# Attention steps with both batches in the same swapped halves, and a weight conversion in two parts

## The chip, the core and the metric

The kernel runs on one core of a Trainium2 chip. Times are device microseconds of one execution; a lower time is better. A core has five engines with queues of their own: PE (TensorE, matmuls, with PEld for its weight loads), DVE (VectorE), ACT (ScalarE), POOL (GpSimd) and SP (SyncE, which issues most DMAs here).

## The reference

Three stages follow each other; all tensors are float32.

```
# linear attention with decay: 2 batches, 8 heads, 12 blocks of 64 positions, head_dim 64
for b in range(12):
    intra = (q_b @ k_b^T * Dmask) @ v_b                # Dmask[i,j] = lam^(i-j) for i >= j
    out_b = intra + (q_b * lam^(pos+1)) @ kv_state
    kv_state = lam^64 * kv_state + (k_b * lam^(63-pos))^T @ v_b
x = out, as 1536 tokens x 512
h = x @ w_in;  x = max(0.01*h, h) @ w_out              # 512 -> 2048 -> 512
h = x @ w_in2                                          # 512 -> 1024
solu = h * softmax(h);  ln = (solu - mean) / sqrt(var + 1e-6) * g_ln
return ln @ w_out2                                     # 1024 -> 512
```

The weights come to the kernel as 64-bit words, which it turns into float32 on the chip.

## The kernel before

Attention is cut into 12 steps, one per block of 64 positions, each for both batches (b = 0, 1). The 8 heads of a batch lie as 4 pairs, the two heads of a pair in the two halves of the 128 partitions. So every attention matmul is 64x64: four of them fit into the 128x128 array at once, one per quadrant (row half of the operands, column half of the output). A step has four kinds, 16 matmuls of each: *scores* (k, q; L169) of the next step, evicted by DVE with the decay mask as r; *xs* (v, r; L201) and *xq* (state, scaled q; L210), which add up in one bank to the step's output x; and *state* (k, v; L183), which DVE adds to the decayed state. On the feature side head h of batch 0 lies in half 1-h, of batch 1 in half h (`d_rows`, L86), so that the same matmul of both batches together fills four quadrants. xs uses two quadrants of one diagonal in each batch; xq of batch 0 writes the rows of xs from other partitions, hence a `pe.drain()` between them (L240).

Steps 0 to 3 run at the start (from L485), one kind after the other. Steps 4 to 11 stand inside the main loop (L561), which goes through 48 units (b, f): three blocks of 512 tokens by 16 slices of w_in and w_out. In unit i PE runs `l1_mm` (w_in, 12 matmuls 128x128 by 512, into a bank hps), the step if i is 4, 7, 10, 13, 17, 21, 25 or 29, and then `l2_mm` of unit i-1 (w_out, 12 matmuls into acc). Matmuls are done in split precision: an operand has a high and a low piece, and the 12 matmuls of `l1_mm` are four with both high pieces, four with the low piece of x, four with the low piece of the weight (L348), in this order. `l1_split` makes Prelu (ACT, L353), the high piece ghi (ACT, L356) and the low piece glo (DVE, L357).

In units 1 to 15 and 35 to 44 the weights of later units are made ready as well. For a weight n: `words` (ACT, L291 and L292) takes two parts out of the 64-bit words; `convert` (DVE, L300 to L302) limits, shifts and joins them to the float32 x; `high` (ACT, L322) rounds x to its high piece and `low` (DVE, L340) subtracts. Unit i does high and low of weight i+1, convert of i+2, words of i+3 and the load of i+5. `scale_k`, `scale_q` and `decay_state` multiply with powers of the decay, on POOL inside the loop.

Each engine runs its instructions in the order in which the program is written (L625 makes that a dependency), so a waiting instruction holds back all behind it on its engine. DMAs go through eight semaphores in turn: a DMA is issued when the eighth before it has landed.

Of the kernel before, what the change touches and what calls it, by code (L numbers as in the profile page):

```python
# [16 lines left out]
P = 128  # L17
CH = 64
NPAIR = 4
NB = 2  # L20
# [21 lines left out]
def fused_kernel(ctx: ExitStack, tc: tile.TileContext, att, vt, tab, cst, w_in, w_out, w_in2, w_out2, out):  # L42
# [42 lines left out]

    def d_rows(b, h):  # L86
        return HALF[h if b else 1 - h]

# [15 lines left out]
    def load_step(s):  # L104

        t = wp.tile([P, 2048], F32, tag="w", name="ldw")
        qkk = t[:, 0:1536].rearrange("p (n c a b) -> p n c a b", n=NB, c=3, a=NPAIR)
        v = t[:, 1536:2048].rearrange("p (n a b) -> p n a b", n=NB, a=NPAIR)
        second = act if s == 0 else sync
        sync.dma_start(out=qkk[:, 0], in_=att[2 * s])  # L110
        for h, queue in ((0, second), (1, sync)):
            queue.dma_start(out=qkk[HALF[h], 1, 0:2], in_=att[2 * s + 1][HALF[1 - h], 0:2])
        second.dma_start(out=v, in_=vt[s])
        sync.dma_start(out=qkk[:, 1, 2], in_=att[2 * s + 1][:, 2])
        ld[s] = (qkk[:, :, 0], qkk[:, :, 1], qkk[:, :, 2], v)

    qk_t = {}

    def load_qk(s):
        if s >= NS:  # L120
            return
        t = qk_t[s] = ap2.tile([P, NB, 2, NPAIR, CH], F32, tag="qk", name="qk")
        sync.dma_start(out=t[:, 0], in_=att[2 * s][:, 0:2])
        for h in range(2):
            sync.dma_start(out=t[HALF[h], 1], in_=att[2 * s + 1][HALF[1 - h], 0:2])

    def load_kv(s):
        if s >= NS:
            return
        t = ap1.tile([P, 2, NB, NPAIR, CH], F32, tag="kv", name="kv")  # L130
        sync.dma_start(out=t[:, 0], in_=att[2 * s : 2 * s + 2, :, 2].rearrange("n p a b -> p n a b"))
        sync.dma_start(out=t[:, 1], in_=vt[s])
        ld[s] = (qk_t[s][:, :, 0], qk_t[s][:, :, 1], t[:, 0], t[:, 1])
# [21 lines left out]
    def decay_state(s, eng):  # L155

        if not 0 < s < NS - 1:
            return
        sd_t[s] = ap1.tile(SHAPE, F32, tag="sd", name="sd")
        n = NB * NPAIR  # L160
        dec = qpow.rearrange("p n a b -> p (n a) b")[:, :, CH - 1 : CH].to_broadcast([P, n, CH])
        st, out_ = (t.rearrange("p n a b -> p (n a) b") for t in (s_t[s], sd_t[s]))
        eng.tensor_tensor(out_, st, dec, op=ALU.mult)

    def scores_mm(s, bank, b, pr):
        q, k = (qk_t[s][:, :, 0], qk_t[s][:, :, 1]) if s >= NPRE else ld[s][0:2]
        for h in range(2):
            d = d_rows(b, h)
            pe.matmul(at(bank, HALF[h], b, pr), k[d, b, pr], q[d, b, pr], start=True, stop=True)  # L169

# [8 lines left out]
    def state_mm(s, bank, b, pr):  # L179

        for h in range(2):
            j = HALF[h]
            pe.matmul(at(bank, d_rows(b, h), b, pr), ld[s][KJ][j, b, pr], ld[s][V][j, b, pr], start=True, stop=True)  # L183

# [11 lines left out]
    def xs_mm(s, bank, b, pr):  # L196

        first = pr == 0 and (b == 0 or isinstance(bank, tuple))
        for h in range(2):
            j = HALF[h]  # L200
            pe.matmul(  # L201
                at(bank, j, b, pr), ld[s][V][j, b, pr], r_t[s][j, b, pr], start=(s == 0 or first), stop=(s == 0)
            )

    def xq_mm(s, bank, b, pr):

        last = pr == NPAIR - 1 and (b == 0 or isinstance(bank, tuple))
        for h in range(2):
            d = d_rows(b, h)
# [9 lines left out]

    def scores(s, bank):  # L220
        each_pair(*((scores_mm, s, bank, b) for b in range(NB)))

    def state(s, bank):
        each_pair(*((state_mm, s, bank, b) for b in range(NB)))

    def x_early(s, bank):
        for b in range(NB):
            each_pair((xs_mm, s, bank, b))
        if s > 0:
            pe.drain()  # L230
            each_pair(*((xq_mm, s, bank, b) for b in range(NB)))

    def step(s, xbank, kbank, rbank):


        more, state_too = s + 1 < NS, s < NS - 1
        each_pair((xs_mm, s, xbank, 0), *([(state_mm, s, kbank, 0)] if state_too else []))
        each_pair((xs_mm, s, xbank, 1), *([(scores_mm, s + 1, rbank, 0)] if more else []))
        each_pair((xq_mm, s, xbank, 1))
        pe.drain()  # L240
        each_pair((xq_mm, s, xbank, 0), *([(state_mm, s, kbank, 1)] if state_too else []))
        if more:
            each_pair((scores_mm, s + 1, rbank, 1))

    def scores_alone(s, rbank):
        each_pair((scores_mm, s, rbank, 0))
        pe.drain()
        each_pair((scores_mm, s, rbank, 1))

# [17 lines left out]

    def load_weights(n):
        if n >= len(order):
            return  # L270
        kind, f = key = order[n]
        t = wp.tile([P, 2, 512, 2], U32, tag="w", name="raww")
        if kind == "a":
            sync.dma_start(out=t.rearrange("p h a b -> p (h a b)"), in_=w_in2[f].bitcast(U32))
        else:
            for i, src in enumerate((w_in[f], w_out[f]) if kind == "io" else (w_out2[f], w_out2[f + 1])):
                sync.dma_start(out=t[:, i].rearrange("p a b -> p (a b)"), in_=src.bitcast(U32))
        raws[n] = t

    BOTH = slice(0, 2)
# [11 lines left out]
    def convert(n, halves=BOTH):  # L294
        if n >= len(order):
            return
        raw = raws[n][:, halves].rearrange("p h a b -> p (h a) b")
        x = xs_t[n][:, halves].rearrange("p h a -> p (h a)")
        xu = x.bitcast(U32)
        dve.tensor_scalar(x, x, HI_MAX, -HI_MAX, op0=ALU.min, op1=ALU.max)  # L300
# [174 lines left out]
    for pr in range(NPAIR):  # L475
        lamj = lams[:, 0, pr : pr + 1].to_broadcast([P, CH])
        dve.tensor_tensor_scan(dmask[:, pr], lamj, delta[:, pr], 0.0, op0=ALU.mult, op1=ALU.add)
    for b in range(NB):
        for pr in range(NPAIR):
            lamd = lams[:, 1 - b, pr : pr + 1].to_broadcast([P, CH])  # L480
            dve.tensor_tensor_scan(qpow[:, b, pr], lamd, zero, 1.0, op0=ALU.mult, op1=ALU.add)
# [3 lines left out]
    scale_k(0, pool)  # L485
    scores(0, sb)
    scores_ev(0, sb)
    state(0, kb)
    x_early(0, xb[0])
    state_ev(0, kb)  # L490
# [9 lines left out]
    scale_k(1, act)  # L500
    scores(1, sb)
    scores_ev(1, sb)
    x_early(1, xb[1])
    state(1, kb)
    low(0, IN)
# [8 lines left out]
    decay_state(2, pool)  # L514
    scores(2, sb)
    scores_ev(2, sb)
    low(0, OUT)
    scale_q(3, pool)
    x_early(2, xb[0])
    scores(3, sb)  # L520
    state(2, kb)
    scores_ev(3, sb)
# [5 lines left out]
    words(1, OUT)  # L528
    x_early(3, xb[1])
    decay_state(3, pool)  # L530
# [6 lines left out]
    l1_mm((0, 0), hps[0])  # L537
    state(3, sb)
    convert(1, OUT)
# [21 lines left out]
    for i, u in enumerate(items[1:], 1):  # L561
# [4 lines left out]
        if i == 2:  # L566
            scores_alone(NPRE, spare)
# [119 lines left out]
```

## Time and profile before

| | |
|---|---|
| three runs | 466.72, 466.94, 468.98 us; median 466.94 |
| the profiled execution | 467.06 us, span 465.3 us |
| PE busy | 449.8 us, 97% |
| DVE busy | 262.1 us, 56% |
| ACT busy | 187.2 us, 40% |
| POOL busy | 53.3 us, 11% |
| chain that ended last | PE 90%, DMA 3%, DVE 3%, ACT 1%, issue 1% |

A busy PE is not PE at its peak: the share says only that some matmul was under way. The chain of waits is followed back from the last instruction, at each step to what released it; its shares say what the time went through. Rows of the timeline merge instructions of one kind that follow each other; two rows may overlap.

### The profile page before, as it was taken

Reading aid. Unit: us, or ns where it says so; the run is one execution under the profiler, and the core shown is the slowest. Engines: PE = TensorE matmul, PEld = TensorE weight load, DVE = VectorE, ACT = ScalarE, POOL = GpSimd, SP = SyncE. Lnnn points to the kernel's source line nnn. Section 1 sums busy time; section 2 is a strip of 40 time slices with the busy share of each in tenths; the row PEclk is TensorE's granted clock in tenths of the full one; section 3 lists DMA queues with packets and bytes.
Section 4 is the critical chain, followed back from the end, with each engine's and each line's share of the span. In section 5 each row is a group of like instructions: output and inputs, shape, how many; then the busy total and the mean of one; then the engine's idle time right before and its main releaser. Section 6 shows DMA issues by size and latency. Waiting matters only on the chain.

```text
span 465.3 us, 7890 instructions
## 1 busy us (share of the span) xinstructions
PE 449.8 (97%) x3332; PEld 370.8 (80%) x3332; DVE 262.1 (56%) x417; ACT 187.2 (40%) x311; POOL 53.3 (11%) x57
## 2 busy tenths in 40 slices
PE   6788999999999999999999999999999999999997
PEld 3765788888888888888888888888888888888886
DVE  4697899999832121211131888912877666666651
ACT  3657667557332222122244777622322222222221
POOL 2434041240403030100000000000000000000000
PEclk9798999999999999999999999999999999999999
DMA  8999064931302020100015542000000000000001
GB/s 273 337 350 370 4 229 173 323 118 66 92 0 93 1 92 1 46 0 2 1 48 213 191 180 92 0 0 2 0 24 23 24 23 23 24 23 24 23 24 45
DMA packets 16659, 41.61 MB, mean 89 GB/s; under 512 B 1904, under 2 KB 4976, under 8 KB 16112
## 3 DMA queue, kind: packets, MB, share of 16 engines
q1 hardware_dynamic: 16400, 40.71, 24.9%
q8 instruction: 26, 0.43, 0.4%
q10 hardware_dynamic: 224, 0.39, 0.3%
q14 instruction: 9, 0.07, 0.0%
HBM read 37.95 MB, written 3.15 MB: 88 GB/s over the span
## 4 chain that ended last, share of the span: by engine, by line
PE 90%; DMA 3%; DVE 3%; ACT 1%; issue 1%; SPq 0%; ACTq 0%
PE hps L350 28%; PE acc L366 27%; PE acc L446 14%; PE hps L384 7%; PE aps L384 7%; DMA ldw<-in_att_dram 3%; PE acc L424 2%; PE aps L210 2%; PE aps L201 2%; PE hps L169 1%; DVE raww L301 1%; DVE x L302 1%; ACT wio L322 0%; DVE xlo L260 0%; DVE state L194 0%
## 5 line engine op out<-in xcount | busy, mean ns | idle before, releaser
L350 PE MATMUL hps<-xhi,wio 128*128 128x512 f32 x384 | 104.0, 393 | 3.2 <-ACT wio L322 2.2
L357 DVE TENSOR_TENSOR glo<-hps,ghi 128x512 fp32r<-128x512 f32 x48 | 33.2, 691 | 122.5 <-ACT ghi L356 121.2
L366 PE MATMUL acc<-ghi,wio 128*128 128x512 f32 x384 | 96.0, 392 | 0.0
L350 PEld LDWEIGHTS hps<-xhi,wio 128*128 128x128 f32 x384 | 72.3, 189 | 19.2 <-ACT wio L322 2.6
L353 ACT ACTIVATE hps<-hps 128x512 f32<-128x512 f32 x48 | 28.0, 582 | 143.4 <-PE hps L350 143.4
L366 PEld LDWEIGHTS acc<-ghi,wio 128*128 128x128 f32 x384 | 71.4, 188 | 15.1
L350 PE MATMUL hps<-xlo,wio 128*128 128x512 f32 x192 | 52.3, 395 | 1.2 <-DVE xlo L260 1.2
L366 PE MATMUL acc<-glo,wio 128*128 128x512 f32 x192 | 51.3, 389 | 0.0
L446 PE MATMUL acc<-wb,lnhi 128*128 128x512 f32 (+1 forms) x208 | 46.0, 374 | 0.3 <-ACT lnhi L432 0.3
L350 PEld LDWEIGHTS hps<-xlo,wio 128*128 128x128 f32 x192 | 36.5, 191 | 9.4 <-DVE xlo L260 1.7
L446 PEld LDWEIGHTS acc<-wb,lnhi 128*128 128x128 f32 x208 | 36.9, 188 | 7.4 <-ACT lnhi L432 0.6
L366 PEld LDWEIGHTS acc<-glo,wio 128*128 128x128 f32 x192 | 36.1, 188 | 7.5
L416 POOL TENSOR_TENSOR small<-small,nhalf 128x1 f32<-128x1 f32 x12 | 6.6, 548 | 251.7 <-DVE small L415 243.3
L301 DVE SCALAR_TENSOR_TENSOR raww<-x,raww 128x1024 uint32<-128x1024 uint32 (+1 forms) x26 | 32.0, 1231 | 1.2 <-ACT raww L292 0.3
L302 DVE SCALAR_TENSOR_TENSOR x<-x,raww 128x1024 uint32<-128x1024 uint32 (+1 forms) x26 | 31.6, 1214 | 0.9
L291 ACT ACTIVATE x<-raww 128x1024 f32<-128x1024 f32 (+1 forms) x26 | 27.9, 1073 | 2.2 <-DMA raww<-in_w_in_dram 2.2
L356 ACT CAST ghi<-hps 128x512 fp32r<-128x512 f32 x48 | 28.2, 587 | 1.5
L292 ACT ACTIVATE raww<-raww 128x1024 uint32<-128x1024 uint16 (+1 forms) x26 | 28.0, 1077 | 0.0
L141 POOL TENSOR_TENSOR qk<-qk,qpow 128x512 f32<-128x512 f32 x8 | 12.2, 1525 | 122.5 <-PE hps L169 122.5
L384 PE MATMUL hps<-wa,xhi 128*128 128x512 f32 x96 | 24.2, 394 | 0.0
L384 PE MATMUL aps<-wa,xhi 128*128 128x512 f32 x96 | 24.2, 394 | 0.0
L446 PE MATMUL acc<-wb,lnlo 128*128 128x512 f32 (+1 forms) x104 | 24.0, 373 | 0.0
(82 smaller groups left out, 527.1 us busy)
## 6 DMA issues: line engine op xcount, KB each, us to landing
raww<-in_w_out_dram SPq DMA_DIRECT2D x24, 512.0 KB, 6.8
raww<-in_w_in_dram SPq DMA_DIRECT2D x16, 512.0 KB, 6.8
raww<-in_w_in_dram SPq DMA_DIRECT2D x4, 1024.0 KB, 4.8
out_dram<-osb SPq DMA_DIRECT2D x11, 256.0 KB, 2.0
qk<-in_att_dram SPq DMA_DIRECT2D x8, 256.0 KB, 4.2
qk<-in_att_dram SPq DMA_DIRECT2D x16, 128.0 KB, 4.6
kv<-in_att_dram SPq DMA_DIRECT2D x8, 256.0 KB, 3.0
kv<-in_vt_dram SPq DMA_DIRECT2D x8, 256.0 KB, 3.8
```

The lines of the kernel that those rows point to most:

```text
L141: eng.tensor_tensor(qs_t[s], q, qpow, op=ALU.mult)
L291: act.activation(x, raw[:, :, 1].bitcast(F32), AF.Copy, scale=HI_SCALE)
L292: act.activation(raw[:, :, 0], raw.bitcast(U16)[:, :, 1], AF.Copy, scale=LO_SCALE)
L301: dve.scalar_tensor_tensor(raw[:, :, 0], xu, 3, raw[:, :, 0], op0=ALU.logical_shift_left, op1=ALU.bitwise_or)
L302: dve.scalar_tensor_tensor(xu, xu, 0x80000000, raw[:, :, 0], op0=ALU.bitwise_and, op1=ALU.bitwise_or)
L350: pe.matmul(bank, w[:, s, k], x[b][:, k], start=(i == 0), stop=(i == len(terms) - 1))
L353: act.activation(bank, bank, AF.Prelu, alpha=0.01)
L356: act.copy(ghi, bank)
L357: dve.tensor_tensor(glo, bank, ghi.bitcast(F32), op=ALU.subtract)
L366: pe.matmul(acc[m], w[:, s, m], g, start=(f == 0 and first), stop=(f == NF - 1 and last))
L384: pe.matmul(bank, x[b][:, k, o : o + P], w2_t["a", k, half][:, s], start=(i == 0), stop=(i == len(terms) - 1),)
L446: pe.matmul(po[:, 0:n], x[:, k], w2_t["b", k][:, s, cols], start=(i == 0), stop=(i == len(terms) - 1))
```

## The change

Four things change. (1) Both batches use the same swapped halves: the feature side and the position side of head h lie in half 1-h, so k and v are loaded half by half into the other half (`load_turned`), and q and k of both batches come in one transfer. All of scores and state then use one diagonal of quadrants, all of xs and xq the other. A step is written as xs with state for batch 0, the same for batch 1, xq with the next scores for batch 0, and for batch 1, without drains. In steps 0 to 3 each kind stands alone. (2) `convert` becomes `bits` (limit, shift) and `join`: the second words operation writes 16 bits into the upper word itself, so that one operation less combines two tensors; shift takes its place. In the main loop bits stands ahead of the low piece, join behind. (3) In a step's unit the eviction of the scores stands between bits and low. (4) `decay_state` of steps 5 to 10 moves from POOL to ACT, into the unit after the step.

```diff
-    def d_rows(b, h):
-        return HALF[h if b else 1 - h]
+    def rows(h):
+        return HALF[1 - h]
...
+    def load_turned(s, kj, v, first, second):
+        for h, queue in ((0, first), (1, second)):
+            queue.dma_start(
+                out=kj[rows(h)], in_=att[2 * s : 2 * s + 2, HALF[h], 2].rearrange("n p a b -> p n a b")
+            )
+        for h, queue in ((0, first), (1, second)):
+            queue.dma_start(out=v[rows(h)], in_=vt[s, HALF[h]])
...
+        if eng is act:
+            for pr in range(NPAIR):
+                act.activation(sd_t[s][:, :, pr], s_t[s][:, :, pr], AF.Copy, scale=qpow[:, 0, pr, CH - 1 : CH])
+            return
...
     def step(s, xbank, kbank, rbank):
-        more, state_too = s + 1 < NS, s < NS - 1
-        each_pair((xs_mm, s, xbank, 0), *([(state_mm, s, kbank, 0)] if state_too else []))
-        each_pair((xs_mm, s, xbank, 1), *([(scores_mm, s + 1, rbank, 0)] if more else []))
-        each_pair((xq_mm, s, xbank, 1))
-        pe.drain()
-        each_pair((xq_mm, s, xbank, 0), *([(state_mm, s, kbank, 1)] if state_too else []))
-        if more:
-            each_pair((scores_mm, s + 1, rbank, 1))
+        both(xs_mm, s, xbank, state_mm, s if s < NS - 1 else NS, kbank)
+        both(xq_mm, s, xbank, scores_mm, s + 1, rbank)
...
-        act.activation(raw[:, :, 0], raw.bitcast(U16)[:, :, 1], AF.Copy, scale=LO_SCALE)
+        act.activation(raw.bitcast(U16)[:, :, 2], raw.bitcast(U16)[:, :, 1], AF.Copy, scale=LO_SCALE)
...
         dve.tensor_scalar(x, x, HI_MAX, -HI_MAX, op0=ALU.min, op1=ALU.max)
-        dve.scalar_tensor_tensor(raw[:, :, 0], xu, 3, raw[:, :, 0], op0=ALU.logical_shift_left, op1=ALU.bitwise_or)
-        dve.scalar_tensor_tensor(xu, xu, 0x80000000, raw[:, :, 0], op0=ALU.bitwise_and, op1=ALU.bitwise_or)
+        dve.tensor_scalar(xu, xu, 3, None, op0=ALU.logical_shift_left)
...
+        dve.scalar_tensor_tensor(xu, raw[:, :, 1], 0x80000007, xu, op0=ALU.bitwise_and, op1=ALU.bitwise_or)
...
         l1_split(u, bank)
         high(pair_at(i, 1))
-        low(pair_at(i, 1))
+        if i > 1:
+            bits(pair_at(i, 2))
...
         if s is not None:
             scores_ev(s + 1, spare)
+        low(pair_at(i, 1))
+        if s is not None:
             state_ev(s, aps[1])
...
-            decay_state(s + 1, pool)
         if i - 1 in step_at:
             scale_k(step_at[i - 1] + 1, pool)
+            decay_state(step_at[i - 1] + 1, act)
...
-            convert(pair_at(i, 2))
+            join(pair_at(i, 2))
```

PE, in the step of unit 4 of the kernel before (aps_85 collects x, aps_86 the state, hps_84 the scores; x2 is the pair's two heads):

```order
L201 MATMUL aps_85<-r,kv 64x64 x2
L183 MATMUL aps_86<-kv 64x64 x2
...
L201 MATMUL aps_85<-r,kv 64x64 x2
L169 MATMUL hps_84<-qk 64x64 x2
L210 MATMUL aps_85<-qk,state 64x64 x10
L183 MATMUL aps_86<-kv 64x64 x2
...
L169 MATMUL hps_84<-qk 64x64 x8
L366 MATMUL acc_79<-ghi,wio 128x512
```

The same place of the changed kernel:

```order
L352 MATMUL hps_83<-xhi_94,wio 128x512 x4
L213 MATMUL aps_85<-r,kv 64x64 x2
L195 MATMUL aps_86<-kv 64x64 x2
...
L222 MATMUL aps_85<-qk,state 64x64 x2
L181 MATMUL hps_84<-qk 64x64 x2
...
L368 MATMUL acc_79<-ghi,wio 128x512
```

State now stands beside xs for both batches and the scores beside xq; no kind is left without a partner.

PE at the start, in step 2 of the kernel before (acc_79 and acc_80 hold x of the two batches, aps_85 and aps_86 the scores of step 3):

```order
L201 MATMUL acc_79<-r,ldw 64x64 x8
L201 MATMUL acc_80<-r,ldw 64x64 x8
L210 MATMUL acc_79<-qs,state 64x64 x2
L210 MATMUL acc_80<-qs,state 64x64 x2
...
L169 MATMUL aps_85<-ldw 64x64 x2
L169 MATMUL aps_86<-ldw 64x64 x2
```

And of the changed kernel:

```order
L213 MATMUL acc_79<-r,ldw 64x64 x8
L213 MATMUL acc_80<-r,ldw 64x64 x8
L222 MATMUL acc_79<-qs,state 64x64 x8
L222 MATMUL acc_80<-qs,state 64x64 x8
L181 MATMUL aps_85<-ldw 64x64 x8
L181 MATMUL aps_86<-ldw 64x64 x8
```

xq and the scores alternated between the batches; now one batch follows the other, as with xs.

DVE in unit 5, which has no step, of the kernel before:

```order
L357 TENSOR_TENSOR glo<-hps_84,ghi 128x512
L340 TENSOR_TENSOR wio<-x,wio 128x1024
L300 TENSOR_SCALAR x<-x 128x1024
L301 SCALAR_TENSOR_TENSOR raww<-x,raww 128x1024
L302 SCALAR_TENSOR_TENSOR x<-x,raww 128x1024
```

And of the changed kernel (L292 and L293 are bits, L342 the low piece, L300 join):

```order
L359 TENSOR_TENSOR glo<-hps_84,ghi 128x512
L292 TENSOR_SCALAR x<-x 128x1024
L293 TENSOR_SCALAR x<-x 128x1024
L342 TENSOR_TENSOR wio<-x,wio 128x1024
L300 SCALAR_TENSOR_TENSOR x<-raww,x 128x1024
```

The low piece, second before, is fourth now; two operations on another weight stand ahead of it.

## Rows read from the trace of the kernel before

**Rows 1.** The page, part 1: busy us of each engine, share, instructions.
```profile
PE 449.8 (97%) x3332; PEld 370.8 (80%) x3332; DVE 262.1 (56%) x417; ACT 187.2 (40%) x311; POOL 53.3 (11%) x57
```

**Rows 2.** The chain, around two units: start us, us, what.
```profile
57.01 0.20 PE aps L201 x2
58.10 0.45 PE aps L210 x16
...
59.34 0.47 PE hps L169 x16
...
62.75 2.72 PE hps L350 x12
65.47 2.72 PE acc L366 x12
```

**Rows 3.** The chain, from the start to the fourth unit.
```profile
12.18 5.23 DMA ldw<-in_att_dram
17.43 1.06 ACT ldw L151 x4
...
20.59 1.15 PE acc L201 x32
...
30.89 0.59 ACT hps L353
...
34.71 1.98 DVE raww L301
...
38.27 1.05 ACT wio L322
39.37 4.62 PE hps L350 x12
...
48.57 3.00 PE hps L350 x12
```

**Rows 4.** Timeline of unit 5: start us, us, engine line, operation.
```profile
66.61 1.05 ACT L322 CAST wio<-x 128x1024 fp32r<-128x1024 f32 x1
66.75 0.69 DVE L357 TENSOR_TENSOR glo<-hps,ghi 128x512 fp32r<-128x512 f32 x1 [0.20 <-ACT ghi L356]
...
67.56 1.14 ACT L291 ACTIVATE x<-raww 128x1024 f32<-128x1024 f32 x1
67.69 1.23 DVE L340 TENSOR_TENSOR wio<-x,wio 128x1024 fp32r<-128x1024 f32 x1 [0.25 <-ACT wio L322]
...
68.83 0.69 DVE L300 TENSOR_SCALAR x<-x 128x1024 f32<-128x1024 f32 x1
...
69.56 1.23 DVE L301 SCALAR_TENSOR_TENSOR raww<-x,raww 128x1024 uint32<-128x1024 uint32 x1
69.62 0.87 PEld L350 LDWEIGHTS hps<-xhi,wio 128*128 128x128 f32 x4
```

**Rows 5.** Timeline of DVE, unit 4 and behind.
```profile
60.45 0.68 DVE L177 TENSOR_TENSOR r<-hps,dmask 128x512 f32<-128x512 f32 x1
61.05 0.68 DVE L194 TENSOR_TENSOR state<-aps,sd 128x512 f32<-128x512 f32 x1
...
62.24 1.18 DVE L300 TENSOR_SCALAR x<-x 128x1024 f32<-128x1024 f32 x1
```

**Rows 6.** Timeline of ACT and PE at the start, operations merged.
```profile
12.66 2.01 ACT L151 ACTIVATE ldw<-ldw,dmask 128x64 f32<-128x64 f32 x8
...
13.86 1.97 PE L201 MATMUL acc<-r,ldw 64*64 64x64 f32 x32 [0.34 <-DVE r L177]
16.03 1.13 PE L210 MATMUL acc<-qs,state 64*64 64x64 f32 x32 [0.20 <-ACT ldw L151]
```

**Rows 7.** Stretches: busy us of each engine, PEclk, DMA share, GB/s.
```profile
12.00:16.00 4.00, 3.29 (x60) 2.89 (x60) 3.32 (x9) 2.91 (x11) 1.27 (x1) 0.55 1.06 328
16.00:20.00 4.00, 2.84 (x96) 2.68 (x96) 1.74 (x5) 2.80 (x10) 1.27 (x1) 0.60 1.03 306
40.00:42.00 2.00, 2.00 (x6) 1.51 (x6) 1.71 (x3) 2.00 (x3) 0.00 (x0) 0.50 1.02 416
```

More of the change, by code (lines that the diff above doesn't have):

```diff
@@ L122, in load_qk @@
         t = qk_t[s] = ap2.tile([P, NB, 2, NPAIR, CH], F32, tag="qk", name="qk")
-        sync.dma_start(out=t[:, 0], in_=att[2 * s][:, 0:2])
-        for h in range(2):
-            sync.dma_start(out=t[HALF[h], 1], in_=att[2 * s + 1][HALF[1 - h], 0:2])
+        sync.dma_start(out=t, in_=att[2 * s : 2 * s + 2, :, 0:2].rearrange("n p c a b -> p n c a b"))
     def load_kv(s):
@@ L167, in scores_mm @@
         for h in range(2):
-            d = d_rows(b, h)
-            pe.matmul(at(bank, HALF[h], b, pr), k[d, b, pr], q[d, b, pr], start=True, stop=True)
+            d = rows(h)
+            pe.matmul(at(bank, d, b, pr), k[d, b, pr], q[d, b, pr], start=True, stop=True)
     def scores_ev(s, bank):
@@ L181, in state_mm @@
         for h in range(2):
-            j = HALF[h]
-            pe.matmul(at(bank, d_rows(b, h), b, pr), ld[s][KJ][j, b, pr], ld[s][V][j, b, pr], start=True, stop=True)
+            j = rows(h)
+            pe.matmul(at(bank, j, b, pr), ld[s][KJ][j, b, pr], ld[s][V][j, b, pr], start=True, stop=True)
     def state_ev(s, bank):
@@ L199, in xs_mm @@
         for h in range(2):
-            j = HALF[h]
+            j = rows(h)
             pe.matmul(
-                at(bank, j, b, pr), ld[s][V][j, b, pr], r_t[s][j, b, pr], start=(s == 0 or first), stop=(s == 0)
+                at(bank, HALF[h], b, pr), ld[s][V][j, b, pr], r_t[s][j, b, pr], start=(s == 0 or first), stop=(s == 0)
             )
     def xq_mm(s, bank, b, pr):
-        last = pr == NPAIR - 1 and (b == 0 or isinstance(bank, tuple))
+        last = pr == NPAIR - 1 and (b == NB - 1 or isinstance(bank, tuple))
         for h in range(2):
-            d = d_rows(b, h)
+            d = rows(h)
             pe.matmul(
@@ L218, in each_pair, with alone, both @@
                 mm(s, bank, b, pr)
[L220 to L226, printed above, removed]
+    def alone(mm, s, bank):
         for b in range(NB):
-            each_pair((xs_mm, s, bank, b))
-        if s > 0:
-            pe.drain()
-            each_pair(*((xq_mm, s, bank, b) for b in range(NB)))
+            each_pair((mm, s, bank, b))
+    def both(mm, s, bank, mm2, s2, bank2):
+        for b in range(NB):
+            each_pair((mm, s, bank, b), *([(mm2, s2, bank2, b)] if s2 < NS else []))
     def step(s, xbank, kbank, rbank):
-        more, state_too = s + 1 < NS, s < NS - 1
-        each_pair((xs_mm, s, xbank, 0), *([(state_mm, s, kbank, 0)] if state_too else []))
-        each_pair((xs_mm, s, xbank, 1), *([(scores_mm, s + 1, rbank, 0)] if more else []))
-        each_pair((xq_mm, s, xbank, 1))
-        pe.drain()
-        each_pair((xq_mm, s, xbank, 0), *([(state_mm, s, kbank, 1)] if state_too else []))
-        if more:
-            each_pair((scores_mm, s + 1, rbank, 1))
[L245 to L248, printed above, removed]
+        both(xs_mm, s, xbank, state_mm, s if s < NS - 1 else NS, kbank)
+        both(xq_mm, s, xbank, scores_mm, s + 1, rbank)
     def x_place(s, x):
@@ L266, in fused_kernel, with load_weights @@
     raws, xs_t = {}, {}
-    def load_weights(n):
+    def load_weights(n, halves=(0, 1)):
         if n >= len(order):
             return
-        kind, f = key = order[n]
-        t = wp.tile([P, 2, 512, 2], U32, tag="w", name="raww")
+        kind, f = order[n]
+        t = raws[n] if n in raws else wp.tile([P, 2, 512, 2], U32, tag="w", name="raww")
         if kind == "a":
@@ L485, in fused_kernel @@
     scale_k(0, pool)
-    scores(0, sb)
+    alone(scores_mm, 0, sb)
     scores_ev(0, sb)
-    state(0, kb)
-    x_early(0, xb[0])
+    alone(state_mm, 0, kb)
+    alone(xs_mm, 0, xb[0])
     state_ev(0, kb)
@@ L500, in fused_kernel @@
     scale_k(1, act)
-    scores(1, sb)
+    alone(scores_mm, 1, sb)
     scores_ev(1, sb)
-    x_early(1, xb[1])
-    state(1, kb)
+    alone(xs_mm, 1, xb[1])
+    alone(xq_mm, 1, xb[1])
+    alone(state_mm, 1, kb)
     low(0, IN)
@@ L514, in fused_kernel @@
     decay_state(2, pool)
-    scores(2, sb)
+    alone(scores_mm, 2, sb)
     scores_ev(2, sb)
@@ L518, in fused_kernel @@
     scale_q(3, pool)
-    x_early(2, xb[0])
-    scores(3, sb)
-    state(2, kb)
+    alone(xs_mm, 2, xb[0])
+    alone(xq_mm, 2, xb[0])
+    alone(scores_mm, 3, sb)
+    alone(state_mm, 2, kb)
     scores_ev(3, sb)
@@ L528, in fused_kernel @@
     words(1, OUT)
-    x_early(3, xb[1])
+    alone(xs_mm, 3, xb[1])
+    alone(xq_mm, 3, xb[1])
     decay_state(3, pool)
@@ L537, in fused_kernel @@
     l1_mm((0, 0), hps[0])
-    state(3, sb)
+    alone(state_mm, 3, sb)
     convert(1, OUT)
@@ L566, in fused_kernel @@
         if i == 2:
-            scores_alone(NPRE, spare)
+            alone(scores_mm, NPRE, spare)
         if s is not None:
```

44 lines of the change are left out of this document (26 added, 18 removed).

## The prediction

> **What bounds the kernel now.** I read the page first: TensorE (PE) is busy in 97% of the span, DVE in 56%, ACT in 40% [rows 1]. So one asks where PE waits, and what it issues that could be shorter. The chain of waits answers both. From 48.57 us on it is PE alone: a unit of w_in matmuls takes 2.72 us, a unit of w_out matmuls 2.72, and between some of them stands an attention step, from 57.01 to 59.34 + 0.47 = 59.81, 2.80 us [rows 2]. Before 48.57 the chain runs through DMA, ACT and DVE [rows 3]. The change works on both stretches, so the sum has four terms: the steps, the weight pieces, the start up to the first unit, and the way from there to the fourth unit.
>
> **The steps.** A step issues 64 small matmuls, each as two instructions. Where only one batch's heads are in flight (two tiles of the array), 16 instructions take 0.45 to 0.47; the interleaved sections hold 32 instructions between 57.01 and the 0.45 row at 58.10, twice, that is 64 in 1.09 with the lead of 0.15, so 0.47 for 32 [rows 2]. The change pairs xs with state and xq with scores, for both batches. Two halves of 16 alone (0.45 + 0.47) become part of a paired section and go at half the price: −0.47; the drain and the refill behind it go too (from 58.55 to 59.34 is 0.79, of which 0.47 is the paired section itself, so 0.31). That is −0.78 for each of the 7 full steps. The last one has nothing to pair with and loses its drain alone, −0.31. Sum −5.8. All of this lies on the chain, since PE has no gap there. If the new pairs shared a quadrant the −0.47 would be lost, 7 × 0.47 = 3.3; they don't, as xs and xq use one diagonal and state and scores the other.
>
> **The weight pieces.** The conversion of a weight had TENSOR_SCALAR, SCALAR_TENSOR_TENSOR, SCALAR_TENSOR_TENSOR (0.69, 1.23, 1.23) and gets two TENSOR_SCALAR and one of the others. DVE isn't the bound, so less work there earns nothing by itself; its place does matter. The first two (bits) now stand ahead of the low piece (L340), and the next unit's third group of matmuls waits for that piece. In a unit without a step, with 65.47 as the end of its w_in matmuls, glo starts at 66.75, the low piece at 67.69 (waiting for ACT), and PE loads the third group's weights at 69.62 [rows 2, 4]. Before, the low piece was written at 67.69 + 1.23 = 68.92, 0.70 early. Now: glo leaves the engine after 0.60 (the spacing of two such operations [rows 5]), at 67.35; the clamp takes 0.73 to the next that depends on it (68.83 to 69.56 [rows 4]), 68.08; the shift is taken at the clamp's 0.61 to 0.73, so 68.75; and 1.23 more is 69.98. PE stalls 69.98 − 69.62 = 0.36. That happens in units 3, 5, 6, 8, 9, 11 and 12: 7 × 0.36 = +2.5. In step units the step itself (2.03 now) covers it. A shift of uint32 is not in the trace. Its nearest rows are the clamp, 0.69, and the operations with two inputs, 1.23 [rows 4]; I take the clamp, which has the same opcode, shape and single SBUF source. At the other end the stall is 0.54 longer, 7 × 0.54 = +3.8. A low end also has to stand: if the clamp and shift cost less one after the other than 0.73 and 0.67, the term shrinks towards +1.0; it can't become a gain.
>
> The Trainium skill (VectorE: DVE Perf Modes, The perf-mode tier table) says that a one-source operation of 4-byte numbers inside SBUF runs at two elements a cycle and one with two sources at one; it lists no shift. The clamp's 0.69 against 1.23 agrees; by the rule the shift is at the cheap end.
>
> ACT's second words operation now waits for its first: about 0.1 more, the overlap that ACT's operations have without a wait (66.61 + 1.05 = 67.66, the next begins at 67.56 [rows 4]). The decay on ACT is four operations of 128 columns, some 0.3 each by the 64-column ones (2.01 for 8 [rows 6]): 1.2 in the unit after a step. With Prelu and ghi (0.59 each [rows 3]), high (1.05) and two words (1.14 each [rows 4]), 4.5, that fills 5.7 of a unit's 5.8 (5.44 and the stall), so it is hidden, by 0.1; if not, Prelu, glo and the low piece slip by what is over. On POOL the decay's removal frees time that nothing waits for. The loads of later steps are the same bytes in as many transfers, and have three units to land.
>
> **The start, up to the end of the first w_in unit (30.89 before).** Two things are later. First, both halves of k now have to land before any of it is scaled on ACT. The last piece of step 2's k landed at 17.41; ACT then scaled 4 pieces in 1.06 [rows 3]. Now v comes last and k a little earlier, with more and smaller packets ahead, so I leave 17.4; but all 8 pieces are scaled behind it, 2.01 [rows 6]. So x_hi, the DVE work behind it and the matmuls at 20.59 start 1.0 later, at 21.6. (Bounds: 0 if k lands 1.0 earlier, 2 if the smaller packets cost another 1.0.)
>
> Second, the attention of steps 0 to 3 loses its four tiles: scores, state and xq were interleaved over both batches and are now each alone, as xs always was. What that costs hangs on TensorE's clock. The granted clock was 0.55 in 12 to 16 us and 0.60 in 16 to 20, i.e. 1.2 GHz of 2.4 nearly throughout, although PE was busy in 3.29 and 2.84 of the 4 us [rows 7]. At 1.2 GHz a two-tile group of 32 took 1.97 (xs), a four-tile one 1.13 (xq) [rows 6]. What PE did in the stretch after which the clock did not rise was mostly xs, two tiles wide; before it rose it did three four-tile groups in a row. In the changed kernel no four-tile group is left there. So I expect it to stay at 1.2 GHz through the whole of the attention. Behind 21.6 stand xs(2), xq(2), scores(3), state(2), xs(3), xq(3): six groups at 1.97 less the 0.3 of the last instruction's own length, 1.7, are 10.2; with 0.3 to the evictions, the first w_in unit starts at 32.1. A unit that began at 1.2 GHz is the one of 39.37 (0.50 in 40 to 42): its 12 full-width matmuls took 4.62, the clock being back for the last of them [rows 3, 7]. At that price the unit ends at 36.7, +5.8.
>
> **From there to the fourth unit.** At 34.71 the SCALAR_TENSOR_TENSOR beside POOL's work took 1.98 [rows 3]; a TENSOR_SCALAR beside POOL took 1.18 [rows 5] and without it 0.69. So the weights of the third unit come 0.8 to 1.3 earlier: −1.0. At 39.37 that unit ran at 1.2 GHz after PE had waited for it; now the wait is 1.0 shorter, and it should run at 2.4, but ACT's high and four words operations (five of 1.05 to 1.14, 5.4 from 38.27) hold back Prelu. Then Prelu, ghi and glo (1.8), the bits (1.35) and the score eviction (0.7) end 9.3 after high's start; before it was 48.57 − 38.27 = 10.3 [rows 3]. Another −1.0. Sum −2.0; bounds 0 and −3.
>
> **Sum.** The profiled execution took 467.06 us (span 465.3 and 1.8 around it), 0.1 above the median of 466.94. 467.06 − 5.8 + 2.5 + 5.8 − 2.0 = **467.6 us**.
>
> **Rivals.** (1) *The clock comes back in the two-tile stretch.* PE is busy there without a gap from about 13.9, which speaks for it; that it was also busy 3.29 of 4 us in 12 to 16 and nothing rose speaks against. Then the six groups take 0.94 each, 5.6, hardly more than before, when xs was two tiles wide and had to wait for evictions between; only the 1.0 of the scaling is left: 467.06 − 5.8 + 2.5 + 1.0 − 2.0 = 462.8. The Trainium skill (TensorE: Matmul & The Clock Gate, What's actually happening) has the gate follow how busy PE was, and doesn't say how a half-filled array counts; read as plain time, it gives this rival. (2) *It comes back part-way*, behind two or three of the six: 464 to 466. (3) *Slower: the shift runs at one element a cycle.* Place: unit by unit, between glo and the low piece; price +3.8 over the forecast, 471.4. It decides from a shift of about 1.0: then 7 × 0.3 more takes the forecast over the bound below. For it: a bit operation in the place of an arithmetic one; against: the clamp's row. DVE beside POOL (1.18 for a clamp) would work through the same door, in three of the seven units. (4) *The steps gain only their drains*: +3.3, 470.9; nothing in the rows speaks for it.
>
> **Chances.** Forecast 0.52 (its own range 465.5 to 469.3), rival 1 0.25, rival 2 0.12, rivals 3 and 4 0.11. A measurement of this kernel can't tell less than about 0.5%, 2.3 us, from no change: faster means below 464.6, slower above 469.3. Faster: nearly all of rival 1, a third of rival 2, a little of the forecast: 0.32. Slower: rivals 3 and 4 with the forecast's upper end: 0.16. Same: 0.52. The range reaches from rival 1 to the forecast with half of the shift's price: 462.3 to 470.0.
>
> **What would show it.** A step of 2.0 us between two units (chain). In units 5, 6, 8, 9, 11 and 12 a wait of PE's weight load for the low piece of 0.3 to 0.4, and a w_in unit of 3.1 instead of 2.7; a shift of 0.69. Four decay operations on ACT, the next Prelu unmoved. The granted clock at half from about 12 us until the first w_in unit, which ends near 36.7; full speed there instead, and an end near 32, is rival 1. Wrong altogether would be a wait that I haven't named in units 4 to 13, where PE has no gap now, or a first w_in unit later than 38.

## The result, and the profile after

The changed kernel takes **473.5 us** (median of 6 runs, 471.5 to 476.2); the kernel before, on the same chip, 467.1 (6 runs). The ratio is 1.0136, 95% interval 1.0102 to 1.0169: slower by 6.4 us, above my forecast of 467.6 and outside its range of 462.3 to 470.0. The profiled executions are further apart, 476.19 to 467.06, the changed kernel's being the slowest of its six, and their spans differ by 474.4 − 465.3 = 9.1. So the stretches read below add up to 9.1, which is 2.7 more than the medians differ by.

The page, part 1, of the changed kernel, to be read against [rows 1]:

```profile
PE 455.0 (96%) x3332; PEld 372.7 (79%) x3332; DVE 245.5 (52%) x417; ACT 227.6 (48%) x335; POOL 43.0 (9%) x51
```

DVE lost 16.6 us of work, as the change meant it to. ACT gained 40.4. The decay that moved there is 7.7 of it (24 operations); the rest has another source. The groups of ACT's instructions by line and shape show it (operation, output<-input, count | busy us, mean ns | idle before). First the kernel before, then the changed one:

```profile
L292 ACT ACTIVATE raww<-raww 128x1024 uint32<-128x1024 uint16 x22 | 25.3, 1151 | 0.0
```

```profile
L285 ACT ACTIVATE raww<-raww 128x1024 uint16<-128x1024 uint16 x22 | 56.1, 2548 | 0.7
...
L284 ACT ACTIVATE x<-raww 128x1024 f32<-128x1024 f32 x22 | 25.3, 1152 | 0.0
```

The second words operation has the same input and as many elements; only its output is 16 bits wide now, one in every 8 bytes. It takes 2.55 us where it took 1.15. The first words operation, beside it, is unmoved.

What that does to ACT as a whole is seen in one stretch, from the first w_in matmul of unit 4 to that of unit 13: nine units, three steps. The views are busy times (us, then PE, PEld, DVE, ACT, POOL with counts, PEclk, DMA share, GB/s), of the kernel before and of the changed one:

```profile
54.13:112.16 58.03, 57.76 (x602) 47.85 (x600) 53.41 (x55) 39.87 (x49) 16.23 (x12) 1.00 0.52 182
```

```profile
62.56:123.87 61.31, 58.86 (x602) 45.14 (x600) 46.26 (x54) 55.36 (x61) 10.10 (x9) 1.00 0.48 172
```

With the shorter steps PE needs 9 x 5.44 + 3 x 2.02 = 55.0 us for this stretch. ACT has 55.4 us to do in it, where it had 39.9. ACT became as full as PE in these units, and the stretch took 61.3, longer than either engine's work, since the two wait for each other in turn. One round of that, in the chain of waits of the changed kernel (start us, us, what):

```profile
70.65 3.01 PE hps L352 x12
73.69 0.59 ACT hps L355
...
74.79 1.05 ACT wio L324
75.84 1.18 ACT sd L170 x4
77.02 1.05 ACT x L284
78.09 2.55 ACT raww L285
80.64 0.49 ACT hps L355
81.15 0.60 ACT ghi L358
81.77 0.69 DVE glo L359
82.46 0.61 DVE x L292
...
83.71 1.23 DVE wio L342
84.98 1.20 PE hps L352 x4
```

In the kernel before, this part of the chain was PE alone [rows 2]. Now it leaves PE at 73.69 and comes back at 84.98. Prelu at 80.64 stands behind the long words operation; ghi, glo, clamp and shift (L292, L293) and the low piece are late behind it, and PE waits for the low piece. The same round begins again at 94.23 and 114.82.

What PE's weight load waited for, 54 to 135 us, in the changed kernel (us in total, times, longest):

```profile
PEld hps L352 <- ACT x L284: 4.4, 1, 4.4
PEld hps L352 <- ACT wio L324: 3.3, 3, 1.1
PEld hps L352 <- DVE wio L342: 3.1, 7, 0.6
PEld hps L352 <- issue: 1.8, 4, 0.5
```

The single wait of 4.4 belongs to the unit ahead of unit 4 (below); the others stand in the rounds of the loop. The kernel before has no row with w_in's matmuls in this view. The steps themselves did what they should; the chain of the changed kernel around a full step, where no weights are converted, and the last step:

```profile
148.92 2.72 PE hps L352 x12
...
153.66 2.95 PE acc L368 x12
...
223.68 1.08 PE aps L213 x32
224.76 0.93 PE aps L222 x32
225.69 2.95 PE acc L368 x12
```

From 151.64 to 153.66 is 2.02 for a full step (2.80 before [rows 2]), and the last one takes 2.01.

The greater part of the loss stands ahead of unit 4. Units count from 0, so the fourth unit is unit 3. The chain of the changed kernel from the start to the fourth unit, against [rows 3]:

```profile
9.91 8.39 DMA ldw<-in_att_dram
18.32 2.02 ACT ldw L159 x8
...
22.43 1.97 PE acc L213 x32
24.40 1.37 PE acc L222 x26
...
33.10 2.50 ACT raww L285
35.60 0.59 ACT hps L355
...
48.10 2.56 ACT raww L285
50.66 0.49 ACT hps L355
...
54.56 5.39 PE hps L352 x12
```

The last load of step 2's k lands at 18.30, 0.9 later than before. Prelu of the first unit starts at 35.60 (30.89 before), that of the third at 50.66 (44.02), both straight behind a words operation of 2.5. The third unit's matmuls had ended at 46.56, so it was ACT alone that held Prelu back there. The first unit's end only at 35.57, with the granted clock at half (0.50 in 33 to 35 us), so there the words operation isn't all that was late. The fourth unit's matmuls begin at 54.56, 6.0 later than before, and take 5.39 for 3.00, since the clock is at half there. Busy times of two stretches, columns as above:

```profile
16.00:20.00 4.00, 4.00 (x106) 4.00 (x103) 1.23 (x3) 1.68 (x7) 1.26 (x1) 0.65 1.07 236
...
54.00:60.00 6.00, 5.44 (x13) 4.32 (x14) 2.68 (x3) 2.31 (x2) 0.00 (x0) 0.52 0.01 3
```

The first w_in matmul of unit 4 thus comes at 62.56, where it came at 54.13: +8.4. This is not a sharp number: the first two experiments have the same program up to unit 4, and their profiles reach it 3.4 apart. From there to unit 14 the loss is 3.3 more, with 3.1 gained in four steps inside it; the four later steps give 2.6 back.

### The profile page after: what moved, and what is told of

Read it like the earlier page. It is cut to its first block, busy times and chain, and to the rows that moved or that the text cites. A ratio compares the mean times of both kernels' runs of the same rounds, so it can differ in the third digit from the quotient of the medians.

```text
span 474.4 us, 7903 instructions
## 1 busy us (share of the span) xinstructions
PE 455.0 (96%) x3332; PEld 372.7 (79%) x3332; DVE 245.5 (52%) x417; ACT 227.6 (48%) x335; POOL 43.0 (9%) x51
## 4 chain that ended last, share of the span: by engine, by line
PE 81%; ACT 8%; DVE 4%; DMA 4%; issue 2%; ACTq 0%; DVEq 0%
PE hps L352 24%; PE acc L368 23%; PE acc L448 14%; PE hps L386 7%; PE aps L386 7%; ACT raww L285 3%; DMA ldw<-in_att_dram 2%; PE acc L426 2%; PE aps L213 2%; ACT x L284 1%; PE aps L222 1%; DMA raww<-in_w_out_dram 1%; DVE wio L342 1%; ACT hps L355 1%; DVE x L292 1%
## 5 line engine op out<-in xcount | busy, mean ns | idle before, releaser
L352 PE MATMUL hps<-xhi,wio 128*128 128x512 f32 x384 | 107.3, 402 | 8.2 <-DVE r L189 4.0
L355 ACT ACTIVATE hps<-hps 128x512 f32<-128x512 f32 x48 | 29.7, 620 | 116.8 <-PE hps L352 116.8
L285 ACT ACTIVATE raww<-raww 128x1024 uint16<-128x1024 uint16 (+1 forms) x26 | 61.5, 2365 | 0.8
L300 DVE SCALAR_TENSOR_TENSOR x<-raww,x 128x1024 uint32<-128x1024 uint32 (+1 forms) x26 | 30.2, 1160 | 1.4 <-ACT raww L285 1.1
L406 ACT ACTIVATE e<-hps,small 128x512 f32<-128x512 f32 x12 | 8.2, 685 | 35.6 <-DVE small L404 35.6
L451 ACT COPY osb<-acc 128x512 f32<-128x512 f32 (+1 forms) x13 | 7.2, 554 | 35.9 <-PE acc L448 35.9
```

What stands on the lines that cost most here:

```text
L285: act.activation(raw.bitcast(U16)[:, :, 2], raw.bitcast(U16)[:, :, 1], AF.Copy, scale=LO_SCALE)
L300: dve.scalar_tensor_tensor(xu, raw[:, :, 1], 0x80000007, xu, op0=ALU.bitwise_and, op1=ALU.bitwise_or)
L352: pe.matmul(bank, w[:, s, k], x[b][:, k], start=(i == 0), stop=(i == len(terms) - 1))
L355: act.activation(bank, bank, AF.Prelu, alpha=0.01)
```

## The experiments

All times are medians; a ratio is to the kernel before on the same chip in the same series, whose median was 467.2 to 467.8. The theory: the 16-bit words operation made ACT late. The rivals: the loads and the two-tile attention at the start; the order on VectorE (bits ahead of the low piece); the decay on ACT.

**The old conversion in the changed kernel.** `words` and `convert` as before, `bits` left out, `convert` in join's place.

```diff
-        act.activation(raw.bitcast(U16)[:, :, 2], raw.bitcast(U16)[:, :, 1], AF.Copy, scale=LO_SCALE)
+        act.activation(raw[:, :, 0], raw.bitcast(U16)[:, :, 1], AF.Copy, scale=LO_SCALE)
...
-        if i > 1:
-            bits(pair_at(i, 2))
...
-            join(pair_at(i, 2))
+            convert(pair_at(i, 2))
```

> The changed kernel with the conversion of the kernel before: the second words operation writes 32 bits again, and clamp and the two operations with two inputs stand together behind the low piece; steps, loads and the decay on ScalarE stay. Theory (the second words operation, 2.5 us where 1.1 was, makes ScalarE late in units 1 to 13 and at the start): the 6.5 us lost between units 4 and 14 go, and 2 to 4 of the 8.4 lost up to unit 4, so 463 to 465 us, the operation at 1.1. Rival (the start's loads and two-tile attention make the 8.4): unit 4 still begins 8 us later than before and the time is 467 or more. Rival (four decay operations on ScalarE): waits stay in the units behind a step, 468 or more.

462.1 us, 0.9896 [0.9867, 0.9926]. The first w_in matmul of unit 4 begins at 53.04, 1.1 before that of the kernel before, and the next run, which is the same up to there, has it at 56.40, where the changed kernel has 62.56. So loads and two-tile attention are not what made most of the 8.4. More of the start came back than my theory had (2 to 4 us).

**The same with the decay on POOL.** What is left of the change are halves, steps and the place of the evictions.

```diff
             scale_q(s + 1, pool)
+            decay_state(s + 1, pool)
...
-            decay_state(step_at[i - 1] + 1, act)
```

> As the run before, with decay_state back on GpSimd in the step's unit: only loads, halves and steps of the change are left. Theory: within 0.5 us of the run before, since 1.2 us of decay is hidden once the words operation is short again (my sum had 0.1 to spare). Rival (decay on ScalarE costs): 1 to 3 us faster than the run before.

467.3 us, 0.9988 [0.9970, 1.0007]: 5 us slower than the run before. This was neither what my theory nor what the rival had. The spans of the two profiles differ by 6.2: 3.4 of that lie ahead of unit 4 (56.40 against 53.04), where no decay has moved yet, and 2.8 behind it. These 2.8 are what the decay's move, which I had priced at nothing, is seen to carry. The timeline behind step 4 shows how (idle before and its releaser in brackets), first with the decay on POOL, then on ACT:

```profile
64.51 1.06 POOL L175 TENSOR_TENSOR sd<-state,qpow 128x512 f32<-128x512 f32 x1 [1.76 <-DVE state L206]
...
65.53 2.63 POOL L161 TENSOR_TENSOR kv<-kv,dmask 128x256 f32<-128x256 f32 x2
...
66.15 1.53 DVE L294 SCALAR_TENSOR_TENSOR raww<-x,raww 128x1024 uint32<-128x1024 uint32 x1
...
67.72 1.53 DVE L295 SCALAR_TENSOR_TENSOR x<-x,raww 128x1024 uint32<-128x1024 uint32 x1
...
70.38 1.20 PE L343 MATMUL hps<-xhi,wio 128*128 128x512 f32 x4 [0.68 <-ACT wio L315]
```

```profile
60.68 1.20 POOL L161 TENSOR_TENSOR kv<-kv,dmask 128x256 f32<-128x256 f32 x2 [1.29 <-DMA kv<-in_att_dram]
...
62.46 1.23 DVE L294 SCALAR_TENSOR_TENSOR raww<-x,raww 128x1024 uint32<-128x1024 uint32 x1
...
63.72 1.23 DVE L295 SCALAR_TENSOR_TENSOR x<-x,raww 128x1024 uint32<-128x1024 uint32 x1
```

Without the decay, scaling k is done before DVE's two operations begin, and they take 1.23 each. With it, they run beside POOL and take 1.53, the clamp 1.17 for 0.83; the rounded weight is late and PE waits 0.68 for its high piece. From 60 to 135 us PE waited 2.8 us for such pieces in the run with POOL, 0.3 in the run before. The kernel before ran beside POOL in the same way [rows 5], but its step was 0.78 longer and its conversion began earlier against the next unit. The rest isn't settled: the first unit already starts at 29.30 in this profile and at 27.49 in the other, and the third then runs for the most part with the granted clock at half (0.50 in 44 to 46 us; 1.00 in the other from 40 to 46), behind the same wait of 1.77 us of PE, though up to there the two programs are the same. The times of the two runs don't overlap (460.6 to 464.4, 465.0 to 468.3) and their medians are 5.2 apart, so chance in two profiles need not be all of it.

**The new conversion alone in the kernel before.** The words line and `convert` (clamp, shift, join, all behind the low piece) of the changed kernel.

```diff
-        act.activation(raw[:, :, 0], raw.bitcast(U16)[:, :, 1], AF.Copy, scale=LO_SCALE)
+        act.activation(raw.bitcast(U16)[:, :, 2], raw.bitcast(U16)[:, :, 1], AF.Copy, scale=LO_SCALE)
...
+        dve.tensor_scalar(xu, xu, 3, None, op0=ALU.logical_shift_left)
+        dve.scalar_tensor_tensor(xu, raw[:, :, 1], 0x80000007, xu, op0=ALU.bitwise_and, op1=ALU.bitwise_or)
```

> The kernel before with only the new conversion (the words operation that writes 16 bits, clamp, shift and one join, all behind the low piece). Theory: ScalarE has 0.59 + 0.60 + 1.05 + 1.05 + 2.5 = 5.8 us to do in a unit of 5.44 without a step, and the start has long words too: 470 to 474 us. Rival (the loss comes from loads, steps or the order of bits): 466 to 468, since one operation with two inputs less can only help VectorE.

472.7 us, 1.0091 [1.0055, 1.0126]: one operation less on DVE, and 4 to 5 us slower. The time is within my theory's range, but the place isn't the one that it gave first, the units of the loop: nearly all of the loss stands ahead of unit 4 (59.74 for 54.13). Units 4 to 13 take 58.22, as before with 58.03: with steps of 2.80 and the decay on POOL, ACT's 52.31 us of work fit into the stretch. It takes the shorter steps and ACT's decay besides for the long words operation to delay the loop.

**The operation by itself.** Nothing but the forms, one after the other.

> Leaves the whole computation out and runs the words operation by itself, three times in each form of 128x1024: 32 bits written into the same or another tile, 16 bits at a stride of 8 bytes into the same or another tile, at 4 bytes, without a gap, and 128x512 of the two forms of the kernels; then a shift and two such scalings on VectorE. Theory (16-bit output at a stride is slow in itself): 2.3 to 2.5 us at 8 bytes in either tile, 1.1 with 32 bits. Rival (the write into the word that is being read is what costs): 1.1 in another tile. Rival (contention with the loads and VectorE in the loop): 1.1 for all forms here. If the write's width alone decides, the form without a gap is slow as well.

The timeline of the second of three rounds, in which nothing is transferred (DMA share 0.00 from 20 to 34 us): 32 bits into another tile and into the same tile, 16 bits at 8 bytes into the same tile (the changed kernel's form) and into another at two places, 16 bits at 4 bytes, and 16 bits without a gap:

```profile
21.61 1.10 ACT L70 ACTIVATE oth<-raw 128x1024 uint32<-128x1024 uint16 x1
22.74 1.10 ACT L71 ACTIVATE raw<-raw 128x1024 uint32<-128x1024 uint16 x1
23.87 2.47 ACT L72 ACTIVATE raw<-raw 128x1024 uint16<-128x1024 uint16 x1
26.09 2.51 ACT L73 ACTIVATE oth<-raw 128x1024 uint16<-128x1024 uint16 x1
28.35 2.51 ACT L74 ACTIVATE oth<-raw 128x1024 uint16<-128x1024 uint16 x1
30.89 1.34 ACT L75 ACTIVATE oth<-raw 128x1024 uint16<-128x1024 uint16 x1
32.11 1.08 ACT L76 ACTIVATE u16c<-raw 128x1024 uint16<-128x1024 uint16 x1
```

The form alone makes the 2.5: with no load and no other engine at work, in either tile. Width alone doesn't (1.08 without a gap), stride alone doesn't (1.10 with 32 bits at 8 bytes); both together do.

**The cheap words operation in the changed kernel.** One line of it undone; the join then takes unrounded low bits.

```diff
-        act.activation(raw.bitcast(U16)[:, :, 2], raw.bitcast(U16)[:, :, 1], AF.Copy, scale=LO_SCALE)
+        act.activation(raw[:, :, 0], raw.bitcast(U16)[:, :, 1], AF.Copy, scale=LO_SCALE)
```

> The changed kernel, only the second words operation writes 32 bits into the lower word, as before the change; the join then takes the three low bits from the unrounded word, so that rounding is left out. Everything else of the change is in. Theory (the 16-bit write alone made the loss): 461 to 463 us, like the run with the old conversion. Rival (bits ahead of the low piece costs 7 times 0.36, as I had predicted, or more beside GpSimd): 464.5 or more.

464.7 us, 0.9946 [0.9926, 0.9967]. The width of one output is worth 8.8 us of the changed kernel's time, more than all of its loss. In this run join doesn't wait for the second words operation either; that this isn't what counts, the run with more work for ACT shows below. The rival is right about the rest. PE's waits, 60 to 135 us, in this run:

```profile
PEld hps L352 <- DVE wio L342: 2.1, 6, 0.4
PEld hps L352 <- ACT raww L285: 1.2, 3, 0.4
...
PEld hps L352 <- issue: 0.4, 1, 0.4
```

Six waits of 0.35 for the low piece are the 0.36 that I had worked out. The other four, 0.4 each, I had not named: behind a step the next w_in unit writes the bank that held the scores, and their eviction (L189) now stands behind bits on DVE. Behind step 4 it ends at 63.13, later than the words operation that the view names (63.01), and those matmuls begin at 63.28.

**The same with clamp and shift behind the low piece.**

```diff
         high(pair_at(i, 1))
-        if i > 1:
-            bits(pair_at(i, 2))
...
         low(pair_at(i, 1))
+        if i > 1:
+            bits(pair_at(i, 2))
```

> The run with the 32-bit words operation and one operation less (464.7 us; rounding left out as there), with clamp and shift behind the low piece. Theory (TensorE's waits for the low piece, six of 0.35 in that run's trace, come from the order alone): 462 to 463 us. Rival (they come from ScalarE): 464.7.

460.2 us, 0.9850 [0.9833, 0.9868], the lowest median of all (4 runs), though with the rounding left out. Both kinds of waits are gone, and units 4 to 13 hold no gap of PE:

```profile
54.59:110.31 55.72, 55.72 (x602) 46.18 (x600) 47.69 (x55) 42.81 (x61) 8.76 (x9) 1.00 0.52 190
```

In the run with bits ahead this stretch took 58.04, so the order costs 2.3 in three rounds.

**More work for ACT, nothing else.** The run with the old conversion; behind the first words operation stands the same operation over a quarter and once more over the whole.

```diff
         act.activation(x, raw[:, :, 1].bitcast(F32), AF.Copy, scale=HI_SCALE)
+        m = x.shape[1] // 4
+        act.activation(x[:, 0:m], raw[:, 0:m, 1].bitcast(F32), AF.Copy, scale=HI_SCALE)
+        act.activation(x, raw[:, :, 1].bitcast(F32), AF.Copy, scale=HI_SCALE)
```

> The run with the old conversion (462.1 us), with more work for ScalarE and nothing else: the first words operation stands twice, once over a quarter and once over the whole, some 1.05 + 0.3 = 1.35 us more per weight, as much as the 16-bit write took. Theory (only ScalarE's time counts: three units then hold 3 x 5.8 + 1.2 + 0.6 = 19.2 us of it, where PE needs 3 x 5.44 + 2.02 = 18.3): 470 to 475 us. Rival (the strided write or the order on VectorE does the harm): 462 to 466.

470.9 us, 1.0077 [1.0054, 1.0100]: 8.8 us over the run with the old conversion, from about 1.5 us more per weight, as much as the 16-bit write costs. Units 4 to 13 look like the changed kernel's; ACT has 56.7 us of work there, against the 55.0 that PE needs:

```profile
57.47:118.13 60.66, 56.97 (x602) 45.67 (x600) 51.22 (x55) 56.73 (x79) 8.42 (x9) 1.00 0.48 174
```

So it is ACT's time that counts; neither the memory word written, nor a change in what join waits for, nor the order on DVE is needed for a loss of this size.

**The changed kernel with the decay on POOL.** The edit of the second run, made in the changed kernel.

> The changed kernel with decay_state back on GpSimd in the step's unit. Theory (ScalarE is over-full by 19.2 to 18.3 per three units, of which the decay is 1.2): the waits for Prelu in units 5 to 14 shrink by most of 6.5 us, but decay on GpSimd costs 0.8 to 0.9 per step as it did with the old conversion (four times), so 469 to 472 us. Rival (decay on ScalarE is hidden, as my sum had it): 473.5 or, with the cost on GpSimd, 477.

469.2 us, 1.0034 [1.0015, 1.0053]: 4.3 faster than the changed kernel. ACT's work in units 4 to 13 falls to 52.26 and the stretch to 58.25. Of the 5.0 between the spans of the two profiles, 3.4 lie between units 4 and 14 (66.36 for 69.78) and 1.6 ahead of unit 4, where nothing differs. So the move that gains 2.8 with a short words operation costs 3.4 with the long one.

**The decay on ACT in the kernel before.**

```diff
-            decay_state(s + 1, pool)
...
             scale_k(step_at[i - 1] + 1, pool)
+            decay_state(step_at[i - 1] + 1, act)
```

> The kernel before with decay_state on ScalarE alone (eight operations of 64 columns, in the unit behind the step). Theory (with a step of 2.8 the conversion beside GpSimd's work is in time, no gap of TensorE stands there): no difference, 467 to 468 us. Rival (decay on ScalarE frees VectorE from GpSimd and is a gain in itself, as the 5 us between the two runs with the old conversion say): 463 to 465.

468.5 us, 1.0030 [1.0014, 1.0046]: no gain, a slight loss, of which 1.4 is seen between units 4 and 14 (67.85 for 66.49). The move pays only where the step is short and ACT has room.

**The low piece ahead of the scores' eviction.** In the run with the old conversion and the decay on POOL:

```diff
         high(pair_at(i, 1))
+        low(pair_at(i, 1))
...
             scores_ev(s + 1, spare)
-        low(pair_at(i, 1))
-        if s is not None:
             state_ev(s, aps[1])
```

> The run with the old conversion and decay on GpSimd (467.3 us), with the low piece ahead of the eviction of the scores again, as in the kernel before. Theory (GpSimd's decay costs there because VectorE is late: with a step of 2.0 it waits idle for the scores at 61.4 and does the low piece, 1.23, only behind them, so that the conversion ends 1.2 later beside GpSimd's work, and the next unit's high piece is late by 0.7): the waits for the high piece behind steps 4, 7 and 10 go, 2 to 3 us, 464 to 465. Rival (decay on GpSimd is slow by itself): 467.

469.6 us, 1.0050 [1.0030, 1.0071]: slower by 2 to 3, so my account of that run was wrong in this part. PE's waits, 60 to 135 us:

```profile
PE hps L343 <- ACT wio L315: 2.8, 4, 0.7
PE hps L343 <- DVE r L189: 1.3, 4, 0.4
```

The waits for the high piece stayed at 2.8, and four new ones came, for the bank of the scores. With a step of 2.0 the eviction is urgent; the change's third part, which had it ahead of the low piece, is needed.

**Pairs at the start.** The run with the old conversion, steps 0 to 2 in pairs (step 2 is shown).

```diff
...
-    alone(xs_mm, 2, xb[0])
-    alone(xq_mm, 2, xb[0])
-    alone(scores_mm, 3, sb)
-    alone(state_mm, 2, kb)
+    both(xs_mm, 2, xb[0], state_mm, 2, kb)
+    both(xq_mm, 2, xb[0], scores_mm, 3, sb)
...
```

> A version meant to beat both: the run with the old conversion, with the attention of steps 0 to 2 in pairs of kinds that use different quadrants (xs with state, xq with the next scores or with state), four tiles wide again. Theory (TensorE is on the path there, six groups of which two are saved at 0.5 to 1.0): 1 to 2.5 us faster than 462.1. Rival (loads and the scaling of k bound the start): 462, or slower if xs waits for state's k.

461.7 us, 0.9871 [0.9843, 0.9898]. Against the run without pairs (0.9896) this can't be told from no change: four tiles for these kinds at the start gain nothing that these runs can show. Both versions beat both kernels.

**Pairs, and the low piece ahead of the eviction.** The low piece moved as two runs above, but in the kernel with pairs, where the decay is on ACT.

> A version meant to beat all: old conversion, decay on ScalarE, pairs at the start, and the low piece ahead of the eviction of the scores. Theory (VectorE's conversion then ends 1.2 earlier in a step's unit, and the waits of 0.3 to 0.7 for the high piece in units 6 to 14, 1.5 in all, go): 460 to 460.5 us. Rival (decay on ScalarE already covers it): 461.7.

464.7 us, 0.9949 [0.9932, 0.9966]: 3 us worse than without the edit, where I had expected a gain of 1 or no change. The same four waits for the scores' bank stand in its trace, 1.3 us in all. The version to keep is the old conversion with the rest of the change.

## Why the prediction was wrong

**The step that failed** is the price of ACT's second words operation: "about 0.1 more, the overlap that ACT's operations have without a wait". Measured: 1.4 more per weight, 2.55 for 1.15. I had taken its duration from the row of before [rows 4], which has another output: 32 bits, not 16 at a stride. Of an operation whose output form changes, the trace of before shows no row, and I should have bounded it from both sides as I did for the shift. The account built on it, 5.7 us of ACT in a unit of 5.8, "hidden, by 0.1", shows how near the edge it was: 1.4 more is 7.1. What follows when it doesn't fit I had written down ("Prelu, glo and the low piece slip by what is over"), but I gave it neither a price nor a chance. The Trainium skill (ScalarE: Activation LUTs, What ACT_TABLE_LOAD costs) puts ScalarE's operations at one element a cycle for every function, by its formula an estimate of 1.0 to 1.1 here; the rows with 32 bits or without a gap agree (1.08 to 1.10), the changed kernel's form doesn't (2.5), and the measurement decides.

**The steps**, −5.8: right. −0.78 for each full step in the chain, −0.31 for the last (2.32 before).

**The weight pieces**, +2.5: right in mechanism and size where ACT isn't late: six waits of 0.35 for the low piece without the long write. The low end that I gave it, +1.0, has no working. The shift takes 0.69 by itself, so the rival of a slow shift (471.4) falls; that the total came out near its number has another cause. Not named were the waits for the scores' bank.

**The start**, +5.8, then −2.0: the end of the first w_in unit came at 35.60, near my 36.7, but by luck. The unit began at 29.79, not at 32.1, and its last groups then ran at half the clock, beside a words operation that ended at the same moment. In the run with the cheap words operation it ended at 33.60, 2.7 later than before, and unit 4 came only 1.0 later. The 1.0 for scaling all of k behind the load was right (two-tile xs at 21.69 there, 20.59 before; in the changed kernel's profile the load also landed later, and xs began at 22.43). From the end of the first unit to the fourth the changed kernel needed 1.3 more than before (18.96 for 17.68), not 2.0 less; with the cheap words operation it was 1.7 less (15.97), so that term holds where ACT isn't late.

That the clock stays at 1.2 GHz through the two-tile attention was wrong: it rose at 18.8, inside a stretch in which PE was busy throughout with two-tile work (4.00 of 4 us, 16 to 20), and fell again at 22.2, when PE had waited 2 us for the scores' eviction. It rose once more at 25.6 (0.60 in 24 to 26, 1.00 in 26 to 28), behind two of the six groups, as rival 2 had it; in the profile with the old conversion it stayed at 1.00 from 20 us on, as rival 1 had it. Without the long write the time is 464.7, where rival 2 put it, 464 to 466, though the four waits for the scores' bank are in it, which no rival had.

**The decay**: its 1.2 on ACT was right (1.18). "Frees time that nothing waits for" was wrong: once steps are short, POOL's work beside DVE's conversion is on the path, and the move was worth 2.8 us of PE's waits with the old conversion, where ACT has room. It had none in the changed kernel.

**What would make it wrong**: I had named a wait in units 4 to 13 that I hadn't listed. That is what came: Prelu behind the words operation.

What stays open: the way to unit 4 differs by up to 3.4 us between profiles of programs that are the same up to there (53.04 and 56.40), so differences of that size ahead of unit 4 aren't put down to any edit, and of the changed kernel's 8.4 only what exceeds them is put down to the long write. Why a narrow write at a stride is slow was not looked into.

## What to carry to other kernels

An edit that saves an operation on one engine by changing the output form of an instruction on another has two prices; measure the new form alone before counting on it. Add up each engine's work over one whole round of the loop, against the bound engine's: where the sum comes within a few per cent of it, as ACT's did here, every term of that sum needs a row of its own. A part of a change can be worth its price only beside another one (the decay's move, behind unit 4: −2.8, +1.4 or +3.4 us), so undo parts in the changed kernel and also try them alone in the old one.

## What the runs showed of the hardware that was not expected

- ScalarE, 128x1024 from uint16 at 8 bytes: 1.10 us with 32-bit output at 8 bytes, 1.08 with 16-bit output without a gap, 1.34 with 16 bits at 4 bytes, 2.5 with 16 bits at 8 bytes.
- VectorE ran a shift of 128x1024 uint32 in 0.69 us, as fast as the clamp, both alone; beside POOL the shift took up to 1.67 in the run with the cheap words operation.
- TensorE's granted clock rose after a stretch of attention that filled half the array only (0.50 in 12 to 16 us, 1.00 from 18.8 to 22.2). Of two runs with the same start, the third unit ran at 1.00 in one and for the most part at 0.50 in the other, behind the same wait of 1.77 us of PE.
